# Retention and a bilinear FFN on one core: slots 6 to 23 transposed by DMA pair by pair, and two blocks of the first tile in 256-column halves

## The chip, the cores and the metric

The kernel runs on one core of a Trainium2 chip. The metric is the device time of one execution in microseconds; lower is better. Times of several runs are given by their median. A profile of one execution shows what each engine did: TensorE (PE, with its weight loads as PEld), VectorE (DVE), ScalarE (ACT), GpSimd (POOL), and SyncE (SP), which here issues nearly all DMAs.

## The reference

Two steps. A retention recurrence over 4 batches, 8 heads, 768 positions and head size 64, then a bilinear FFN over its 3072 rows of 512 columns.

```
state = gamma[h] * state + k_t (outer) v_t          # per batch and head, 64 x 64
y_t   = scale * q_t @ state
...
x   = y as [3072, 512]
out = ((x @ w_a) * (x @ w_b)) @ w_out               # w_a, w_b: 512 x 1536, w_out: 1536 x 512
```

Inputs and the output are float32.

## The kernel before, in words

**Slots and tiles.** The 3072 rows are 24 slots of 128 positions, 6 to a batch. The FFN works on tiles of slots, `TILES = [4, 2, 2, 2, 2, 4, 4, 4]`: the first tile is 512 columns wide (slots 0 to 3), the next four 256 (4 to 11), the last three 512. For a tile `J`, `ffn_a(J, ft)` and `ffn_g(J, ft)` compute one of 12 blocks of 128 rows of x @ w_a and x @ w_b, each with four matmuls (`KT`), into one PSUM bank; ACT copies the first into `asb` (L507), DVE multiplies the second by it into `ht` (L516). `ffn_out(J, i)` then makes the 128 output rows of slot `i` of the tile with 12 matmuls of 512 columns (L541), ACT copies them to `osb`, and a store is kept in `held`; `store()` issues it on SP at the start of the next FFN step.

**Retention.** It is computed in chunks of 64 positions. For each slot q and k are loaded (`load_slot`, L83; three DMAs of 256 KB on SP, for k, q and v), scaled with decay tables and cast to bf16 into `kqb` (`scaled`, L207, on POOL for slots from 6 on), and v is cast into `vb` (L224). q and k are then needed transposed, as `kqT`. Slots 0 to 5 take a path of their own (`casts2`, `flip2`, `scores2` and so on), which the change does not touch. For the slots from 6 on, `turn(new, old)` runs the retention of a pair of slots: the chunk states of the new pair (`chunk_states`, L264, which reads `kb` and `vb`), its scores (`scores`, L287, which reads `kqT`), and, for the pair before it, the part across chunks (`inter`, L328, which reads `kqT`) and within them (`intra`, L340, which reads `vb`), which make x for the FFN.

**Who transposes.** `ON_PE = 8`. Slots from 8 on are transposed by DMA: `casts(t)` issues the transpose on SP (L227) behind the scaling, and behind it on SP the three loads of slot t + 3 (L231). Slots 6 and 7 are transposed by TensorE: `flip(t)` runs eight transposes of 128x128, four for k and four for q (L236, L238), into a PSUM bank, and DVE copies the result into `kqT` (L240).

**Order.** Each engine's instructions run in the order in which they are written (`seq`), so each queue is one line of waiting. SP's first loads are the list `LOADS`: ten of its entries at the start, the rest (`issue_loads(100)`, L595) during the first tile, ending with slots 6, 7, 8, 9 and 10. The dictionary `ahead` (L636) says which of `casts`, `flip` and `turn` is written ahead of which FFN step: (1, 6) is block 6 of tile 1, (0, "o", 1) the second output block of tile 0. All 12 blocks of tile 1 come before the output blocks of tile 0, then those of tile 1, and from tile 2 on each tile's blocks are followed by its outputs.

**Buffers.** The raw loads of k, q and v lie in 3 buffers each, one to a pair of slots; `kqb`, `vb` and `kqT` have 6 each, so slot t takes over what slot t - 6 leaves; PSUM gives 3 banks to the tag `ff`, which the FFN blocks, the output blocks and `flip` share.

Of the kernel before, what the change touches and what calls it, by code (L numbers as in the profile page):

```python
# [10 lines left out]
BF16 = mybir.dt.bfloat16  # L11
# [3 lines left out]

TILES = [4, 2, 2, 2, 2, 4, 4, 4]
PAIRS = 3
ON_PE = 8


LOADS = "k0 q0 k1 q1 v0 v1 w0 w1 w2 w3 w4 k2 q2 v2 w5 o0 o1 o2 o3 o4 o5 s6 s7 s8 s9 s10".split()


@with_exitstack
def kernel(
# [10 lines left out]
    nc = tc.nc  # L36
    P = 128
    B, H, S, D = q.shape
    NCH = S // P
    HP = H // 2  # L40
    DM = H * D
    DFF = moe_w_a.shape[1]
    KT = DM // P
    NFT = DFF // P
    NSLOT = B * NCH
# [14 lines left out]
    tra = ctx.enter_context(tc.tile_pool(name="tra", bufs=4))  # L60
# [3 lines left out]
    psff = ctx.enter_context(tc.tile_pool(name="psff", bufs=3, space=bass.MemoryType.PSUM))  # L64
# [7 lines left out]
    def seq(bi):  # L72
        ins = bi.ins
        prev = last.get(ins.engine)
        if prev is not None:
            tc.add_manual_dep(ins, prev.name, nosync, reason="program order")
        last[ins.engine] = ins
        return bi


    raws, wst, whole = {}, {}, {}

    def load_slot(t):  # L83
        b, ci = divmod(t, NCH)
        for nm, src in (("k", k), ("q", q), ("v", v)):
            if t % 2 == 0:
                whole[nm] = raw.tile([P, 2, H, D], F32, tag=nm + "f", name=nm + "f")
            raws[nm, t] = whole[nm][:, t % 2]
            s = src[b, :, ci * P : (ci + 1) * P, :].rearrange("h p d -> p h d")
            seq(nc.sync.dma_start(out=raws[nm, t], in_=s))  # L90

    def load_pair(nm, u):
        src = {"k": k, "q": q, "v": v}[nm]
# [18 lines left out]

    pending = list(LOADS)

    def issue_loads(n):
        for _ in range(min(n, len(pending))):
            what = pending.pop(0)
            if what[0] in "kqv":
                load_pair(what[0], int(what[1:]))
            else:  # L120
                {"s": load_slot, "w": load_w, "o": load_o}[what[0]](int(what[1:]))
# [11 lines left out]
    ident = const.tile([P, P], BF16, name="ident")  # L133
# [43 lines left out]
    wa_bf = wpool.tile([P, KT, DFF], BF16, name="wa_bf")  # L177
    wb_bf = wpool.tile([P, KT, DFF], BF16, name="wb_bf")
    wo_bf = wpool.tile([P, NFT, DM], BF16, name="wo_bf")

    def cast(engine, dst, src):
        if engine is nc.scalar:
            seq(nc.scalar.copy(dst, src))  # L183
        else:
            seq(engine.tensor_copy(dst, src))  # L185
# [11 lines left out]
    kb, qb, vb, kqT, aT = {}, {}, {}, {}, {}  # L197
# [9 lines left out]
    def scaled(eng, t, i):  # L207
        ktab, qtab = tabs[0] if t < 2 * PAIRS else tabs[1]
        dst, src, tab = kqb[t][:, i], raws["kq"[i], t], (ktab, qtab)[i][:, t % NCH]
        dst = dst.rearrange("p hp r d -> p r hp d")  # L210
        src = src.rearrange("p (r hp) d -> p r hp d", r=2)
        tab = tab.rearrange("p (r hp) o -> p r hp o", r=2).to_broadcast([P, 2, HP, D])
        seq(eng.tensor_tensor(dst, src, tab, op=ALU.mult))  # L213

    def new_nat(t):
        kqb[t] = nat.tile([P, 2, HP, 2, D], BF16, tag="kqb", name="kqb")
        kb[t], qb[t] = kqb[t][:, 0], kqb[t][:, 1]
        vb[t] = nat.tile([P, H, D], BF16, tag="vb", name="vb")

    def casts(t):  # L220
        new_nat(t)
        scaled(nc.gpsimd, t, 0)
        scaled(nc.gpsimd, t, 1)
        cast(nc.gpsimd, vb[t], raws["v", t])  # L224
        if t >= ON_PE:
            kqT[t] = tra.tile([P, 2, HP, P], BF16, tag="kqT", name="kqT", bufs=6)
            seq(nc.sync.dma_start_transpose(  # L227
                out=kqT[t].rearrange("p a b c -> p (a b) c"),
                in_=kqb[t].rearrange("p a hp r d -> p (a hp r d)")))
            if t + 3 < NSLOT:  # L230
                load_slot(t + 3)  # L231

    def flip(t):
        tp = psff.tile([P, 2, HP, P], BF16, tag="ff", name="tp")
        for hp in range(HP):
            seq(nc.tensor.transpose(tp[:, 0, hp, :], kb[t][:, hp, :, :], ident))  # L236
        for hp in range(HP):
            seq(nc.tensor.transpose(tp[:, 1, hp, :], qb[t][:, hp, :, :], ident))  # L238
        kqT[t] = tra.tile([P, 2, HP, P], BF16, tag="kqT", name="kqT", bufs=6)
        seq(nc.vector.tensor_copy(kqT[t], tp))  # L240

    def half(i):
        return slice(64 * i, 64 * i + 64)
# [238 lines left out]
    def xcols(J, kt, c0, c1):  # L482
        if J < 2:
            return xt[J][:, c0 // P : c1 // P, kt, :]
        return xt[J][:, kt, c0:c1]
# [8 lines left out]

    asbs = {}

    def ffn_a(J, ft, c0=0, c1=None):
        c1 = TILES[J] * P if c1 is None else c1
        if J not in ht:
            ht[J] = htp.tile([P, NFT, 4 * P], BF16, tag="ht", name="ht")  # L500
        fs = slice(ft * P, (ft + 1) * P)
        a = psff.tile([P, 4 * P], F32, tag="ff", name="a")[:, : c1 - c0]
        for kt in range(KT):
            seq(nc.tensor.matmul(a, wa_bf[:, kt, fs], xcols(J, kt, c0, c1),  # L504
                                 start=(kt == 0), stop=(kt == KT - 1)))
        asb = asbs[J, ft, c0] = asbp.tile([P, 4 * P], BF16, tag="asb", name="asb")[:, : c1 - c0]
        seq(nc.scalar.copy(asb, a))  # L507

    def ffn_g(J, ft, c0=0, c1=None):
        c1 = TILES[J] * P if c1 is None else c1  # L510
        fs = slice(ft * P, (ft + 1) * P)
        g = psff.tile([P, 4 * P], F32, tag="ff", name="g")[:, : c1 - c0]
        for kt in range(KT):
            seq(nc.tensor.matmul(g, wb_bf[:, kt, fs], xcols(J, kt, c0, c1),  # L514
                                 start=(kt == 0), stop=(kt == KT - 1)))
        seq(nc.vector.tensor_tensor(ht[J][:, ft, c0:c1], g, asbs.pop((J, ft, c0)), op=ALU.mult))  # L516

    def ffn_ab(J, ft):
        store()
        ffn_a(J, ft)  # L520
        ffn_g(J, ft)
        catch_up(2)
# [67 lines left out]
    leave2(1, (A_, D_))  # L590
    W2 = 2 * P
    ffn_a(0, 0, 0, W2)
    update2(1, 1, False)
    ffn_a(0, 1, 0, W2)
    issue_loads(100)  # L595
    cast_w(1)
    ffn_g(0, 0, 0, W2)
    ffn_a(0, 0, W2, 2 * W2)
    ffn_a(0, 1, W2, 2 * W2)
    ffn_g(0, 1, 0, W2)  # L600
    ffn_g(0, 0, W2, 2 * W2)
    ffn_g(0, 1, W2, 2 * W2)
# [31 lines left out]
    for j in range(NO):  # L634
        cast_o(j)
    ahead = {  # L636
        (1, 6): [(casts, 6)], (1, 9): [(flip, 6), (casts, 7)], (0, "o", 0): [(flip, 7)],
        (0, "o", 1): [(turn, 6, None)], (0, "o", 2): [(casts, 8)], (0, "o", 3): [(casts, 9)],
        (1, "o", 1): [(turn, 8, 6, D_), (casts, 10)],
        (2, 2): [(casts, 11)], (2, 7): [(casts, 12)], (2, "o", 1): [(turn, 10, 8, D_), (casts, 13)],  # L640
        (3, 0): [(casts, 14)], (3, 6): [(casts, 15)], (3, "o", 0): [(turn, 12, 10), (casts, 16)],
# [58 lines left out]
```

## Time and profile before

| | |
|---|---|
| runs | 227.81 us median of 3 (227.33 to 228.07) |
| the profiled execution | 226.77 us, of it 225.1 us span from the first to the last instruction |
| granted TensorE clock | 1.000 |
| DMA | 39.20 MB, mean 174 GB/s over the span |

Engines overlap, so busy times don't add up to the span. The profile counts a matmul as busy until its modelled end, and matmuls are pipelined, so a group's own length is read from the starts of it and of what follows it. Weight loads (PEld) overlap matmuls. A row of the timeline gives the start and the length in us, the engine, the line of the kernel, the operation, what it writes and reads, the shape and a count; in square brackets stands how long the engine was idle ahead of it and what ended that.

### The profile page before, as it was taken

To read this page: it belongs to the slowest core of one execution; us is meant where nothing else is said; L and a number is where in the kernel's file an instruction comes from. 1 tells how busy PE (TensorE), PEld (TensorE's weight loads), DVE (VectorE), ACT (ScalarE), POOL (GpSimd) and SP (SyncE) were. 2 spreads that over 40 slices of the span, in tenths; PEclk is the share of its full clock that TensorE was granted. 3 is DMA by queue.
4 is the path that set the end of the run, shared out by engine and by line. 5 is a ranking of instruction groups with operands and counts; after the bars stand their busy time and mean duration, and the time that the engine had idled before them with its cause. 6 is when DMAs were issued, how large, how long until landed. Compare 5 with 4: busy or idle time off the path is not lost.

```text
span 225.1 us, 6289 instructions
## 1 busy us (share of the span) xinstructions
PE 218.3 (97%) x2632; PEld 131.5 (58%) x2632; DVE 97.4 (43%) x197; ACT 96.1 (43%) x206; POOL 80.0 (36%) x104
## 2 busy tenths in 40 slices
PE   7789999999999999999999999999999999999994
PEld 7567445796546867875885444545444544444444
DVE  3784347554506535462467243544243422333300
ACT  3465335332427326455447433355433354333222
POOL 5677799687544435417019510050000000000000
PEclk9999999999999999999999999999999999999999
DMA  6999999999999999999949893044100012100022
GB/s 186 347 380 382 364 309 406 303 241 219 208 288 231 298 152 207 265 237 167 287 113 206 184 248 67 3 96 143 47 0 0 3 50 93 47 3 1 1 93 93
DMA packets 94012, 39.20 MB, mean 174 GB/s; under 512 B 73888, under 2 KB 89504, under 8 KB 93984
## 3 DMA queue, kind: packets, MB, share of 16 engines
q1 hardware_dynamic: 93840, 38.68, 68.9%
q8 instruction: 20, 0.33, 0.6%
q10 hardware_dynamic: 144, 0.13, 0.2%
q14 instruction: 8, 0.07, 0.1%
HBM read 28.31 MB, written 6.29 MB: 154 GB/s over the span
## 4 chain that ended last, share of the span: by engine, by line
PE 92%; DMA 3%; ACT 1%; POOL 1%; issue 1%; SPq 0%; POOLq 0%
PE o L541 28%; PE g L514 28%; PE a L504 28%; DMA kf<-in_k_dram 3%; PE y L328 1%; POOL kqb L213 1%; PE at L287 1%; PE y L340 1%; PE st L264 1%; PE y L467 1%; PE y L455 1%; PE tp L402 0%; PE st L438 0%; SPq L96 0%; ACT qT L183 0%
## 5 line engine op out<-in xcount | busy, mean ns | idle before, releaser
L516 DVE TENSOR_TENSOR ht<-g,asb 128x256 bf16<-128x256 f32 (+1 forms) x98 | 53.9, 550 | 84.3 <-PE g L514 74.4
L514 PE MATMUL g<-xt,wb_bf 128*128 128x256 bf16 (+1 forms) x392 | 77.6, 323 | 0.1
L504 PE MATMUL a<-xt,wa_bf 128*128 128x256 bf16 (+1 forms) x392 | 77.6, 323 | 0.0
L507 ACT CAST asb<-a 128x256 bf16<-128x256 f32 (+1 forms) x98 | 46.4, 473 | 71.6 <-PE a L504 70.9
L541 PE MATMUL o<-wo_bf,ht 128*128 128x512 bf16 (+2 forms) x312 | 64.4, 363 | 0.0
L504 PEld LDWEIGHTS <-wa_bf 128*128 128x128 bf16 x392 | 38.0, 98 | 24.8 <-DVE xt L185 0.4
L514 PEld LDWEIGHTS <-wb_bf 128*128 128x128 bf16 x392 | 38.3, 98 | 23.9 <-issue 0.2
L541 PEld LDWEIGHTS <-ht 128*128 128x128 bf16 x312 | 28.8, 98 | 30.5
L213 POOL TENSOR_TENSOR kqb<-kf,ktab 128x512 bf16<-128x512 f32 x22 | 22.9, 1045 | 22.3 <-DMA kf<-in_k_dram 19.7
L183 ACT COPY osb<-o 128x512 f32<-128x512 f32 (+2 forms) x25 | 14.1, 565 | 33.4 <-PE o L541 28.1
L185 POOL CAST vb<-vf 128x512 bf16<-128x512 f32 x24 | 14.5, 613 | 38.0 <-PE y L340 24.8
L213 POOL TENSOR_TENSOR kqb<-qf,qtab 128x512 bf16<-128x512 f32 x21 | 22.4, 1067 | 1.8 <-DMA qf<-in_q_dram 1.7
L183 ACT CAST gst<-sums 128x256 bf16<-128x256 f32 x33 | 13.4, 405 | 6.1 <-DVE sums L278 2.8
L278 DVE TENSOR_TENSOR sums<-st,sums 128x256 f32<-128x256 f32 x30 | 12.7, 424 | 1.6
L293 DVE TENSOR_TENSOR aT<-at,mask 128x512 bf16<-128x512 f32 x18 | 11.5, 679 | 0.0
L351 ACT CAST xt<-y 128x512 bf16<-128x512 f32 x16 | 8.5, 584 | 0.0
L490 PE MATMUL idle<-zero 128*128 128x170 bf16 (+1 forms) x56 | 7.2, 295 | 1.1 <-DVE zero L127 1.1
L425 DVE TENSOR_TENSOR aT<-at,mask 128x512 bf16<-128x512 f32 x12 | 7.4, 678 | 0.7 <-PE at L415 0.7
L185 POOL CAST wa_bf<-wsta 128x1024 bf16<-128x1024 f32 (+1 forms) x7 | 6.4, 922 | 2.7 <-DMA wsta<-in_moe_w_a_dram 2.6
L185 POOL CAST wb_bf<-wstb 128x1024 bf16<-128x1024 f32 (+1 forms) x7 | 6.4, 922 | 1.4 <-DMA wstb<-in_moe_w_b_dram 1.4
L185 POOL CAST wo_bf<-wsto 128x1024 bf16<-128x1024 f32 x6 | 6.3, 1044 | 1.7 <-DMA wsto<-in_moe_w_out_dram 0.9
L305 DVE COPY lgr<-bq 128x1 f32<-128x1 f32 x4 | 0.6, 154 | 14.2 <-PE y L328 14.2
(58 smaller groups left out, 95.1 us busy)
## 6 DMA issues: line engine op xcount, KB each, us to landing
out_dram<-osb SPq DMA_DIRECT2D x23, 256.0 KB, 3.4
kf<-in_k_dram SPq DMA_DIRECT2D x18, 256.0 KB, 4.1
qf<-in_q_dram SPq DMA_DIRECT2D x18, 256.0 KB, 4.1
vf<-in_v_dram SPq DMA_DIRECT2D x18, 256.0 KB, 4.5
wsta<-in_moe_w_a_dram SPq DMA_DIRECT2D x6, 512.0 KB, 7.7
wstb<-in_moe_w_b_dram SPq DMA_DIRECT2D x6, 512.0 KB, 7.8
wsto<-in_moe_w_out_dram SPq DMA_DIRECT2D x6, 512.0 KB, 7.8
kf<-in_k_dram SPq DMA_DIRECT2D x3, 512.0 KB, 5.8
```

The source lines that it names most:

```text
L183: seq(nc.scalar.copy(dst, src))
L185: seq(engine.tensor_copy(dst, src))
L213: seq(eng.tensor_tensor(dst, src, tab, op=ALU.mult))
L278: seq(nc.vector.tensor_tensor(new, u[c][:, s], old, op=ALU.add))
L293: seq(nc.vector.tensor_tensor(aT[n][:, r].rearrange("p s h d -> p (s h) d"), at[:, r].rearrange("p s h d -> p (s h) d"), mask.to_broadcast ...
L351: seq(nc.scalar.copy(dst, ys[o][c]))
L425: seq(nc.vector.tensor_tensor(aT[t][:, r], ats[t][r], masks[par].to_broadcast([P, HP, P]), op=ALU.mult))
L504: seq(nc.tensor.matmul(a, wa_bf[:, kt, fs], xcols(J, kt, c0, c1), start=(kt == 0), stop=(kt == KT - 1)))
L507: seq(nc.scalar.copy(asb, a))
L514: seq(nc.tensor.matmul(g, wb_bf[:, kt, fs], xcols(J, kt, c0, c1), start=(kt == 0), stop=(kt == KT - 1)))
L516: seq(nc.vector.tensor_tensor(ht[J][:, ft, c0:c1], g, asbs.pop((J, ft, c0)), op=ALU.mult))
L541: seq(nc.tensor.matmul(o, ht[J][:, ft, i * P : (i + 1) * P], wo_bf[:, ft, c0:c1], start=(ft == 0), stop=(ft == NFT - 1)))
```

## The change

`ON_PE` and `flip` go; `casts` issues a DMA transpose for slots 6 and 7 too. The first list of loads ends with slot 7. From then on the loads go by pairs: behind the transpose of an odd slot t, SP gets the loads of k and q of slots t + 1 and t + 2, then those of v. `load_slot` and `casts` take the names of what they are to handle, and slots 8 and 9 have k and q of both scaled ahead of v. In `casts` the loop over `("kq", "v")` uses the variable `names` again. In `ahead`, slot 7 moves from (1, 9) to (1, 8). For blocks 2 and 3 of the first tile each matmul of 512 columns becomes two of 256, into the two halves of the same bank.

```
-LOADS = "k0 q0 k1 q1 v0 v1 w0 w1 w2 w3 w4 k2 q2 v2 w5 o0 o1 o2 o3 o4 o5 s6 s7 s8 s9 s10".split()
+LOADS = "k0 q0 k1 q1 v0 v1 w0 w1 w2 w3 w4 k2 q2 v2 w5 o0 o1 o2 o3 o4 o5 s6 s7".split()
...
-    def load_slot(t):
+    def load_slot(t, names="kqv"):
         b, ci = divmod(t, NCH)
-        for nm, src in (("k", k), ("q", q), ("v", v)):
+        for nm in names:
...
+    def casts(t, names="kqv"):
+        if "k" in names:
+            new_nat(t)
+            scaled(nc.gpsimd, t, 0)
+            scaled(nc.gpsimd, t, 1)
             kqT[t] = tra.tile([P, 2, HP, P], BF16, tag="kqT", name="kqT", bufs=6)
             seq(nc.sync.dma_start_transpose(
                 out=kqT[t].rearrange("p a b c -> p (a b) c"),
                 in_=kqb[t].rearrange("p a hp r d -> p (a hp r d)")))
-            if t + 3 < NSLOT:
-                load_slot(t + 3)
+            if t % 2 and t + 1 < NSLOT:
+                for names in ("kq", "v"):
+                    load_slot(t + 1, names)
+                    load_slot(t + 2, names)
+        if "v" in names:
+            cast(nc.gpsimd, vb[t], raws["v", t])
...
+    def parts(J, ft, c0, c1):
+        if J == 0 and ft in (2, 3):
+            return [(c0, (c0 + c1) // 2), ((c0 + c1) // 2, c1)]
+        return [(c0, c1)]
...
         for kt in range(KT):
-            seq(nc.tensor.matmul(a, wa_bf[:, kt, fs], xcols(J, kt, c0, c1),
-                                 start=(kt == 0), stop=(kt == KT - 1)))
+            for b0, b1 in parts(J, ft, c0, c1):
+                seq(nc.tensor.matmul(a[:, b0 - c0 : b1 - c0], wa_bf[:, kt, fs], xcols(J, kt, b0, b1),
+                                     start=(kt == 0 and b0 == c0), stop=(kt == KT - 1 and b1 == c1),
+                                     skip_group_check=True))
...
-        (1, 6): [(casts, 6)], (1, 9): [(flip, 6), (casts, 7)], (0, "o", 0): [(flip, 7)],
-        (0, "o", 1): [(turn, 6, None)], (0, "o", 2): [(casts, 8)], (0, "o", 3): [(casts, 9)],
+        (1, 6): [(casts, 6)], (1, 8): [(casts, 7)], (0, "o", 1): [(turn, 6, None)],
+        (0, "o", 2): [(casts, 8, "kq")],
+        (0, "o", 3): [(casts, 9, "kq"), (casts, 8, "v"), (casts, 9, "v")],
```

`ffn_g` is changed as `ffn_a` is.

More of the change, by code (lines that the diff above doesn't have):

```diff
@@ L17 @@
 PAIRS = 3
-ON_PE = 8
-LOADS = "k0 q0 k1 q1 v0 v1 w0 w1 w2 w3 w4 k2 q2 v2 w5 o0 o1 o2 o3 o4 o5 s6 s7 s8 s9 s10".split()
+LOADS = "k0 q0 k1 q1 v0 v1 w0 w1 w2 w3 w4 k2 q2 v2 w5 o0 o1 o2 o3 o4 o5 s6 s7".split()
 @with_exitstack
@@ L88, in load_slot @@
             raws[nm, t] = whole[nm][:, t % 2]
-            s = src[b, :, ci * P : (ci + 1) * P, :].rearrange("h p d -> p h d")
-            seq(nc.sync.dma_start(out=raws[nm, t], in_=s))
+            s = {"k": k, "q": q, "v": v}[nm][b, :, ci * P : (ci + 1) * P, :]
+            seq(nc.sync.dma_start(out=raws[nm, t], in_=s.rearrange("h p d -> p h d")))
     def load_pair(nm, u):
@@ L218, in new_nat @@
         vb[t] = nat.tile([P, H, D], BF16, tag="vb", name="vb")
[L220 to L225, printed above, removed]
+    def casts(t, names="kqv"):
[3 more added lines that the diff above has]
+            scaled(nc.gpsimd, t, 1)
             kqT[t] = tra.tile([P, 2, HP, P], BF16, tag="kqT", name="kqT", bufs=6)
@@ L229, in casts @@
                 in_=kqb[t].rearrange("p a hp r d -> p (a hp r d)")))
-            if t + 3 < NSLOT:
-                load_slot(t + 3)
[L233 to L240, printed above, removed]
+            if t % 2 and t + 1 < NSLOT:
[4 more added lines that the diff above has]
+            cast(nc.gpsimd, vb[t], raws["v", t])
     def half(i):
@@ L513, in ffn_g @@
         for kt in range(KT):
-            seq(nc.tensor.matmul(g, wb_bf[:, kt, fs], xcols(J, kt, c0, c1),
-                                 start=(kt == 0), stop=(kt == KT - 1)))
+            for b0, b1 in parts(J, ft, c0, c1):
+                seq(nc.tensor.matmul(g[:, b0 - c0 : b1 - c0], wb_bf[:, kt, fs], xcols(J, kt, b0, b1),
+                                     start=(kt == 0 and b0 == c0), stop=(kt == KT - 1 and b1 == c1),
+                                     skip_group_check=True))
         seq(nc.vector.tensor_tensor(ht[J][:, ft, c0:c1], g, asbs.pop((J, ft, c0)), op=ALU.mult))
```

## The prediction

> **What bounds the kernel now.** I read the page first: span, busy shares, the slices and the chain of work that ended last.
>
> ```profile
> span 225.1 us, 6289 instructions
> PE 218.3 (97%) x2632; PEld 131.5 (58%) x2632; DVE 97.4 (43%) x197; ACT 96.1 (43%) x206; POOL 80.0 (36%) x104
> ...
> PE   7789999999999999999999999999999999999994
> ...
> PEclk9999999999999999999999999999999999999999
> DMA  6999999999999999999949893044100012100022
> ...
> PE 92%; DMA 3%; ACT 1%; POOL 1%; issue 1%; SPq 0%; POOLq 0%
> ```
>
> TensorE sets the end: it is busy in every slice from the fourth on, its granted clock is full throughout, and the chain is 92% PE. The transfers are busy too, up to about 112 us (the first 20 slices of 5.63 us), but the chain has only 3% of them, all at the start. The view of busy time by windows says the same for the stretch that the change touches:
>
> ```profile
> 42.00:50.00 8.00, 8.00 (x76) 7.10 (x75) 4.09 (x9) 3.36 (x9) 6.24 (x7) 1.00 1.05 239
> 50.00:57.00 7.00, 7.00 (x118) 4.89 (x116) 3.39 (x7) 1.70 (x4) 5.20 (x6) 1.00 1.02 229
> ...
> 85.00:121.00 36.00, 36.00 (x679) 27.46 (x667) 19.03 (x44) 18.98 (x49) 14.21 (x17) 1.00 1.01 209
> ```
>
> The columns are length, busy time of PE, PEld, DVE, ACT and POOL, clock, DMA share, GB/s. PE is busy for all of each window; no other engine reaches 80% on the same terms, save the weight loads, which overlap. So what leaves PE's stream leaves the end, unless a new wait takes its place.
>
> **The change, part by part.** *The 16 transposes of slots 6 and 7 leave PE* (L236, L238). The timeline of PE shows what they take:
>
> ```profile
> 49.81 0.39 PE L236 MATMUL tp<-ident,kqb 128*128 128x128 bf16 x4
> 50.04 0.39 PE L238 MATMUL tp<-ident,kqb 128*128 128x128 bf16 x4
> 50.26 0.60 PE L504 MATMUL a<-xt,wa_bf 128*128 128x256 bf16 x4
> ...
> 52.95 0.39 PE L236 MATMUL tp<-ident,kqb 128*128 128x128 bf16 x4
> 53.17 0.39 PE L238 MATMUL tp<-ident,kqb 128*128 128x128 bf16 x4
> 53.39 2.75 PE L541 MATMUL o<-wo_bf,ht 128*128 128x512 bf16 x12
> 56.08 0.45 PE L264 MATMUL st<-vb,kqb 64*64 64x64 bf16 x32
> 56.35 0.49 PE L287 MATMUL at<-kqT 64*64 64x64 bf16 x32
> ```
>
> Matmuls are pipelined, so starts count, not durations: 50.26 - 49.81 = 0.45 and 53.39 - 52.95 = 0.44, together 0.89 us off PE. The Trainium skill, "TensorE: Matmul & The Clock Gate", section on the PE-mode transpose, puts a 128x128 transpose at about 275 ns in one kernel's context; by that the 16 would be worth an estimated 4.4 us. The starts above stand 56 ns apart, so the trace disagrees and I go by it.
>
> Their two copies on DVE (0.69 us each) leave too. That is worth nothing on the path: DVE is busy 3.39 of 7.00 us there.
>
> ```profile
> L240 DVE COPY kqT<-tp 128x1024 bf16<-128x1024 bf16 x2 | 1.4, 690 | 0.0
> ```
>
> *Halves.* The blocks ft = 2 and 3 of the first tile run 16 matmuls of 512 columns (a and g, 4 each); they become 32 of 256. Both widths stand side by side:
>
> ```profile
> 18.78 1.04 PE L504 MATMUL a<-xt,wa_bf 128*128 128x256 bf16 x8
> 19.65 1.47 PE L514 MATMUL g<-xt,wb_bf 128*128 128x256 bf16 x12
> 20.96 1.89 PE L504 MATMUL a<-xt,wa_bf 128*128 128x512 bf16 x8
> 22.69 1.89 PE L514 MATMUL g<-xt,wb_bf 128*128 128x512 bf16 x8
> ```
>
> 256 columns: (20.96 - 19.65) / 12 = 109 ns. 512 columns: (22.69 - 20.96) / 8 = 216 ns. Two halves cost 218 ns against 216: 16 x 2.6 ns = 0.04 us more. Each half has a weight load of its own (98 ns), which 109 ns still covers. If none of the 16 added loads were covered, they would cost 1.57 us; that is the upper bound, 0 the lower; I take 0.04, since the same form runs at that pace just before.
>
> ```profile
> L504 PEld LDWEIGHTS <-wa_bf 128*128 128x128 bf16 x392 | 38.0, 98 | 24.8 <-DVE xt L185 0.4 <-issue 0.2
> ```
>
> Sum on PE: -0.89 + 0.04 = -0.85 us. Everything else has to stay hidden, and that is the question.
>
> *Slots 6 and 7 by DMA.* The queue SP now issues the transpose of slot 6 (T6) right behind the loads of slot 7, T7 next, and only then the loads of 8 and 9 (k8 q8 k9 q9 v8 v9). T6 and T7 wait for POOL's scaling, and k8 to v9 are queued behind them. The rows of POOL, of SP, and of the transposes before:
>
> ```profile
> 45.40 1.04 POOL L213 TENSOR_TENSOR kqb<-qf,qtab 128x512 bf16<-128x512 f32 x1
> ...
> 48.19 1.04 POOL L213 TENSOR_TENSOR kqb<-qf,qtab 128x512 bf16<-128x512 f32 x1
> 49.18 0.61 POOL L185 CAST vb<-vf 128x512 bf16<-128x512 f32 x1
> ```
> ```profile
> 44.72 0.93 SPq L90 DMA_DIRECT2D vf<-in_v_dram  x1
> ```
> ```profile
> L227 SPq DMA_TRANSPOSE kqT<-kqb x10: 1288/1378/1862, 57.3 to 107.7; - x10
> ...
> DMA to landing us min/median/max: 3.7/4.4/5.5
> ```
>
> SP is free of slot 7's loads at 45.7. q6 is scaled at 46.4, q7 at 49.2; a transpose takes SP 1.4 us and lands 4.4 us (5.5 at most) after its issue starts, in the crowded stretch from 57 to 112 us. So T7 lands at 49.3 + 4.4 = 53.7 (54.8 at most). Its first reader is the score group L287 at 56.35, 0.85 earlier after the change: 55.5. Slack 1.8 us, 0.7 at the worst. Cost 0; without that cover, each us of lateness is a us of PE.
>
> *Slots 8 and 9.* Before, T9 was issued at 62.91. Its new predecessors: loads from 50.7 on. A load lands 4.1 us after issue, and the next ones follow at 0.262 MB / 233 GB/s = 1.13 us each (both from the stretch 57 to 112 us, the loads of k and the summary of the DMA queues):
>
> ```profile
> 62.91 1.33 SPq L227 DMA_TRANSPOSE kqT<-kqb  x1
> ```
> ```profile
> DMA to landing us min/median/max: 3.3/4.1/5.1
> ```
> ```profile
> DMA packets 42462, 12.80 MB, mean 233 GB/s; under 512 B 41303, under 2 KB 41303, under 8 KB 42455
> ```
> ```profile
> 59.62 0.59 ACT L183 COPY osb<-o 128x512 f32<-128x512 f32 x1 [0.71 <-PE o L541]
> 67.68 0.45 PE L287 MATMUL at<-kqT 64*64 64x64 bf16 x32
> ```
>
> k8 lands at 54.8, q9 at 54.8 + 3.4 = 58.2, scaled at 59.2 (1.04 us, the rows of POOL above). T9 also stands behind the store of the second output block, which waits for ACT's copy: 59.62 + 0.59 - 0.85 = 59.4. So T9 is issued at 59.4 and lands at 63.8 (64.9), 3 us before its reader (67.68 - 0.85 = 66.8). In `casts` the loop variable overwrites `names`, so slot 9's v is cast a second time: one more 0.61 us on POOL, where POOL stands idle for 3.00 us:
>
> ```profile
> 63.06 1.04 POOL L213 TENSOR_TENSOR kqb<-kf,ktab 128x512 bf16<-128x512 f32 x1 [3.00 <-DMA kf<-in_k_dram]
> ```
>
> *The later pairs.* Loads ran three slots ahead; now a pair's six are issued behind the last transpose of the pair before, so one link hangs on the next: transpose issue 1.4, first load 4.1, four more (q, k, q, v) 4 x 1.13 = 4.5, then POOL's v, k and q 0.61 + 1.04 + 1.04 = 2.7: 12.7 us a pair. From T9 at 59.4, T17 is issued four links on at 110.2 and lands at 114.6. The readers of slots 10, 12, 14 and 16 are
>
> ```profile
> 84.77 0.44 PE L287 MATMUL at<-kqT 64*64 64x64 bf16 x29
> ...
> 99.19 0.49 PE L287 MATMUL at<-kqT 64*64 64x64 bf16 x32
> ...
> 116.29 0.49 PE L287 MATMUL at<-kqT 64*64 64x64 bf16 x32
> ...
> 120.22 0.21 PE L287 MATMUL at<-kqT 64*64 64x64 bf16 x1
> ```
>
> For slots 16 and 17 that is 120.22 - 0.85 = 119.4, slack 4.8 us over four links, the least of all per link (slots 10 to 15: 83.9 - 76.5 = 7.4 over one, 98.3 - 89.2 = 9.1 over two, 115.4 - 101.9 = 13.5 over three). Cost 0. Its bound the other way: 1.86 for the issue, 5.1 to land, 4 x 0.262 MB / 209 GB/s = 5.0 at the pace of the window 85 to 121, and 2.7 make 14.7 a link; T17 then lands at 59.4 + 58.8 + 5.5 = 123.7, and PE stands for 4.3 us.
>
> The sum: the span becomes 225.1 - 0.85 = 224.25, the profiled execution 226.77 - 0.85 = 225.9. The runs shown have their median 1.04 us above that execution, so 227.81 - 0.85 = 226.96, said as 226.95.
>
> **The rivals.** *The chain of pairs is too long (slower).* The place is the turn of slots 16 and 17 at 119.4. It decides from (119.4 - 59.4 - 4.4) / 4 = 13.9 us a link; each us above costs PE four, and above 14.1 the whole is slower. At the bound of 14.7, 4.3 us: 231.3. For it: the transfers stand at 9 in every slice up to 112 us, so a link may meet stores and transposes in the queue. Against: that load was made by running ahead, and 12.7 leaves 1.2 us a link. Chance 0.08.
>
> *The halves expose their weight loads.* 1.57 instead of 0.04: 227.81 - 0.89 + 1.57 = 228.5. Against: 12 matmuls of that form at 109 ns. Chance 0.08.
>
> *The gain is swallowed by a wait at the next hand-over.* T7, T9 or a cast comes 0.85 us later than PE can use it, past the worst case above, by a delay that the rows don't show: 227.8. For it: T7's slack at the worst is only 0.7. Against: the DMA queue is emptier than before once three slots' loads are gone from it. Chance 0.13.
>
> *The transposes cost more than their starts say.* One by itself takes 0.39 - 3 x 0.056 = 0.22 us (four take 0.39, started 56 ns apart); if what follows had to wait for each to drain, the 16 would be worth 3.5 us: 227.81 - 3.5 + 0.04 = 224.35. Against: the next block's first matmul starts 0.22 us after the second four, as if they flowed on. Chance 0.03. By the page's 275 ns it would be 227.81 - 4.4 + 0.04 = 223.45, which the same row speaks against.
>
> **How the numbers follow.** The forecast has 0.68, and its own range is 226.5 to 227.4: 0.85 with some 0.4 either way for the spread of the runs before (227.33 to 228.07). A measurement here tells about 0.3%, 0.68 us, from no change, and 0.85 is just beyond it. So of the 0.68 I count 0.56 as faster by more than that, 0.11 as within, 0.01 as slower; of the swallowed gain 0.06 within and 0.07 slower; the first two rivals are slower, 0.16, the last faster, 0.03. Faster 0.59, same 0.17, slower 0.24. The range, 226.3 to 228.4, holds nearly all of the forecast and of the swallowed gain and reaches to the exposed halves at 228.5 without all of it; the long chain lies outside.
>
> **What would show it.** Right: no L236 and L238, 18 transposes on SP, the score group of slots 6 and 7 starting 0.8 to 0.9 us earlier with no PE idle before it, and the same lead at 66.8, 84, 98, 115 and 119 us. The halves are right if the 16 blocks of 256 columns start 109 ns apart. The chain is right if T17 lands before 119 us. Wrong: idle time of PE ahead of an L287 or an L264, put down to a transpose's landing or to a cast of vb, or a lead that shrinks from one turn to the next.

## The result and the profile after

The changed kernel takes 226.56 us, median of 10 runs (226.02 to 227.02); the kernel before, run beside it, 227.38 (226.92 to 228.07, 10 runs). The ratio is 0.9964 [0.9949, 0.9978], so the change gains 0.82 us. Ratios leave out runs more than 1.5% above the fastest of their kernel; one run further down, of 233.13 us, is such. The profiled execution of the changed kernel took 226.44 us. Its page:

```profile
span 224.7 us, 6284 instructions
PE 217.7 (97%) x2632; PEld 132.3 (59%) x2632; DVE 96.2 (43%) x195; ACT 96.0 (43%) x206; POOL 80.3 (36%) x105
...
PEclk9999999999999999999999999999999999999999
DMA  6999999998899996999979996974100012100022
...
q8 instruction: 20, 0.33, 0.6%
...
PE 92%; DMA 3%; ACT 1%; POOL 1%; issue 1%; SPq 0%; POOLq 0%
```

The picture is that of before: PE fills the span at full clock, and the chain is 92% PE. PE has the same 2632 matmuls, since 16 transposes went and 16 matmuls came. DVE has two instructions less (the copies of the transposes), POOL one more (the second cast of slot 9's v). The line of q8, a queue that carries instructions, matters further down: 20 packets with 0.33 MB, 16 KB each.

The timeline of PE around the place where the transposes were (columns: start, length, engine, line, operation, tiles, shape, count):

```profile
49.46 0.60 PE L516 MATMUL g<-xt,wb_bf 128*128 128x256 bf16 x4
49.90 0.60 PE L504 MATMUL a<-xt,wa_bf 128*128 128x256 bf16 x4
...
52.08 0.60 PE L516 MATMUL g<-xt,wb_bf 128*128 128x256 bf16 x4
52.52 2.75 PE L544 MATMUL o<-wo_bf,ht 128*128 128x512 bf16 x12
55.20 0.45 PE L257 MATMUL st<-vb,kqb 64*64 64x64 bf16 x32
55.47 0.49 PE L280 MATMUL at<-kqT 64*64 64x64 bf16 x32
```

The FFN blocks follow each other 0.44 us apart without a gap, and the scores of slots 6 and 7 start at 55.47 instead of 56.35: a lead of 0.88 us. The same timeline further on, at the scores (L280) of the later pairs and at the chunk states (L257) of the last:

```profile
66.81 0.45 PE L280 MATMUL at<-kqT 64*64 64x64 bf16 x32
...
98.43 0.49 PE L280 MATMUL at<-kqT 64*64 64x64 bf16 x32
...
115.52 0.49 PE L280 MATMUL at<-kqT 64*64 64x64 bf16 x32
...
119.10 0.32 PE L321 MATMUL y<-kqT,gst 64*64 64x64 bf16 x16
119.30 0.67 PE L257 MATMUL st<-vb,kqb 64*64 64x64 bf16 x20
...
119.86 0.42 PE L280 MATMUL at<-kqT 64*64 64x64 bf16 x28
```

The rows of the kernel before at the last of these turns:

```profile
119.87 0.32 PE L328 MATMUL y<-kqT,gst 64*64 64x64 bf16 x16
120.05 0.35 PE L264 MATMUL st<-vb,kqb 64*64 64x64 bf16 x19
...
120.30 0.44 PE L287 MATMUL at<-kqT 64*64 64x64 bf16 x28
```

Against the rows of before the lead is 0.87 at 66.81, 0.76 at 98.43, 0.77 at 115.52, and 120.30 - 119.86 = 0.44 at the last one. So 0.1 us was lost at the turn of slots 10 and 11 and 0.3 at the turn of 16 and 17. There the chunk states take 0.67 us for 20 matmuls, where the kernel before took 0.35 for 19, and no wait is recorded with them. These leads are counted from the start of the span; the first FFN matmul starts at 17.02 here and at 16.98 before. Counted from that matmul on, the lead is 0.92 at the scores of slots 6 and 7, and PE's last matmul starts 0.49 us earlier than before; a second execution of the changed kernel has 0.55.

The halves, in the same timeline:

```profile
21.00 1.91 PE L504 MATMUL a<-xt,wa_bf 128*128 128x256 bf16 x16
22.75 1.91 PE L516 MATMUL g<-xt,wb_bf 128*128 128x256 bf16 x16
24.49 1.67 PE L504 MATMUL a<-xt,wa_bf 128*128 128x512 bf16 x7
```

(22.75 - 21.00) / 16 = 109 ns each, as in the rows of before.

The timeline of SP, from slot 7's transpose to slot 17's:

```profile
50.34 1.23 SPq L225 DMA_TRANSPOSE kqT<-kqb  x1
...
57.22 3.04 SPq L531 DMA_DIRECT2D out_dram<-osb  x1
60.35 1.31 SPq L225 DMA_TRANSPOSE kqT<-kqb  x1
61.76 0.53 SPq L531 DMA_DIRECT2D out_dram<-osb  x1
62.38 1.31 SPq L225 DMA_TRANSPOSE kqT<-kqb  x1
...
75.27 1.26 SPq L225 DMA_TRANSPOSE kqT<-kqb  x1
...
99.51 1.26 SPq L225 DMA_TRANSPOSE kqT<-kqb  x1
...
112.36 1.24 SPq L225 DMA_TRANSPOSE kqT<-kqb  x1
```

T7 goes out at 50.34 and lands 3.2 us later (the view of that line gives the landing) at 53.5, 2.0 us ahead of its reader. T9 goes out at 62.38, lands at 65.4, 1.4 us ahead. T17 goes out at 112.36, lands at 115.8, 4.1 us ahead. No score group waits for a transpose.

So the open questions were: is it the transposes that bring the gain, and the order of the loads that covers them; what do the halves do; how much room has the chain of pairs; and what is the stop at the turn of 16 and 17?

### The profile page after: what moved, and what is told of

Read it like the earlier page. It is cut to its first block, busy times and chain, and to the rows that moved or that the text cites. A ratio compares the mean times of both kernels' runs of the same rounds, so it can differ in the third digit from the quotient of the medians.

```text
span 224.7 us, 6284 instructions
## 1 busy us (share of the span) xinstructions
PE 217.7 (97%) x2632; PEld 132.3 (59%) x2632; DVE 96.2 (43%) x195; ACT 96.0 (43%) x206; POOL 80.3 (36%) x105
## 4 chain that ended last, share of the span: by engine, by line
PE 92%; DMA 3%; ACT 1%; POOL 1%; issue 1%; SPq 0%; POOLq 0%
PE o L544 28%; PE g L516 28%; PE a L504 28%; DMA kf<-in_k_dram 3%; PE y L321 1%; POOL kqb L212 1%; PE at L280 1%; PE y L333 1%; PE st L257 1%; PE y L460 1%; PE y L448 1%; PE tp L395 0%; PE st L431 0%; SPq L95 0%; ACT qT L182 0%
## 5 line engine op out<-in xcount | busy, mean ns | idle before, releaser
L504 PEld LDWEIGHTS <-wa_bf 128*128 128x128 bf16 x400 | 38.8, 98 | 24.0 <-DVE xt L184 0.4
L516 PEld LDWEIGHTS <-wb_bf 128*128 128x128 bf16 x400 | 39.1, 98 | 23.1 <-issue 0.2
L271 DVE TENSOR_TENSOR sums<-st,sums 128x256 f32<-128x256 f32 x30 | 12.7, 424 | 1.9 <-PE st L257 0.4
```

Source lines behind the costliest of these rows:

```text
L271: seq(nc.vector.tensor_tensor(new, u[c][:, s], old, op=ALU.add))
L504: seq(nc.tensor.matmul(a[:, b0 - c0 : b1 - c0], wa_bf[:, kt, fs], xcols(J, kt, b0, b1), start=(kt == 0 and b0 == c0), stop=(kt == KT - 1 a ...
L516: seq(nc.tensor.matmul(g[:, b0 - c0 : b1 - c0], wb_bf[:, kt, fs], xcols(J, kt, b0, b1), start=(kt == 0 and b0 == c0), stop=(kt == KT - 1 a ...
```

## The experiments: what the gain is made of

Theory: TensorE loses 16 transposes, worth 0.88 us, and the new order of loads is only cover for the two DMA transposes. Rivals: the new order of loads or the halves bring the gain.

**The DMA transposes without the new order.** The kernel before, with slots 6 and 7 transposed by DMA, the loads as they were.

```
-        if t >= ON_PE:
+        if True:
...
-            if t + 3 < NSLOT:
+            if t >= ON_PE and t + 3 < NSLOT:
...
-        (1, 6): [(casts, 6)], (1, 9): [(flip, 6), (casts, 7)], (0, "o", 0): [(flip, 7)],
+        (1, 6): [(casts, 6)], (1, 8): [(casts, 7)],
```

> The kernel before, with slots 6 and 7 transposed by DMA and nothing else moved: the loads of slots 8, 9 and 10 stay ahead of the two transposes in SP's queue, the blocks stay whole. Theory (the transposes are the gain, the order of the loads is their cover): SP is through with those loads at 55.9 us, so T6 is issued there and T7 some 1.5 us later, T7 lands at about 61.5 to 62; the scores of slots 6 and 7 want it at 55.5, so PE stands for some 6 us and the kernel is about 5 us slower than before (+4 to +6.5). Rival (the transposes are worth 0.85 us wherever they stand in the queue): 0.85 us faster than before. Rival (the order of the loads makes the gain, not the transposes): within 0.3 us of before.

Measured: 233.94 us (233.25 to 234.97), ratio 1.0309 [1.0282, 1.0335], 7.0 us slower, more than the 4 to 6.5 expected. Its SP and PE timelines:

```profile
54.50 1.60 SPq L90 DMA_DIRECT2D vf<-in_v_dram  x1
56.20 3.06 SPq L227 DMA_TRANSPOSE kqT<-kqb  x2
```
```profile
55.69 0.45 PE L264 MATMUL st<-vb,kqb 64*64 64x64 bf16 x32
60.23 0.43 PE L287 MATMUL at<-kqT 64*64 64x64 bf16 x16 [4.10 <-DMA kqT<-kqb]
61.07 0.43 PE L287 MATMUL at<-kqT 64*64 64x64 bf16 x16 [0.41 <-DMA kqT<-kqb]
```

Both transposes stand on SP behind the nine loads of slots 8 to 10, go out at 56.2, and PE stands for 4.10 + 0.41 us. The cover is thus the place in the queue. But 4.5 us of standing cost 7.0, in a kernel that also lost the 16 transposes. The windows of this run show one part of the rest (length, busy time of PE, PEld, DVE, ACT, POOL, then the granted clock):

```profile
58.00:60.30 2.30, 0.07 (x4) 0.07 (x8) 0.07 (x1) 0.46 (x2) 1.80 (x3) 0.52 1.28 224
60.30:62.00 1.70, 1.29 (x33) 0.80 (x35) 0.45 (x1) 0.00 (x0) 0.00 (x0) 0.50 1.10 288
62.00:64.00 2.00, 1.78 (x6) 0.64 (x5) 0.84 (x2) 0.00 (x0) 0.00 (x0) 0.50 0.73 164
64.00:66.00 2.00, 2.00 (x9) 0.86 (x8) 0.00 (x0) 0.02 (x1) 1.44 (x2) 0.77 1.13 255
```

The clock is at half some 2 us after PE stopped (56.1), and stays there to about 65, well into the work: (1.7 + 2.0) x 0.50 + 2.0 x 0.23 = 2.3 us more. 4.5 + 2.3 - 0.9 = 5.9 us. That is all that this trace has: counted from the first FFN matmul on, PE's last matmul starts 5.79 us later than before. The rest of the 7.0 lies outside this stretch: the profiled execution took 233.25, the shortest of the four, and its first FFN matmul started at 17.55, 0.57 us later than before.

**The new order without the DMA transposes.** The kernel before with the loads by pairs, slots 6 and 7 still transposed by TensorE (the `flip` entries stay in `ahead`), whole blocks. The order of scalings of slots 8 and 9 is that of the changed kernel.

```
-LOADS = "k0 q0 k1 q1 v0 v1 w0 w1 w2 w3 w4 k2 q2 v2 w5 o0 o1 o2 o3 o4 o5 s6 s7 s8 s9 s10".split()
+LOADS = "k0 q0 k1 q1 v0 v1 w0 w1 w2 w3 w4 k2 q2 v2 w5 o0 o1 o2 o3 o4 o5 s6 s7".split()
...
+            if t >= 8:
...
+            if t % 2 and t + 1 < NSLOT:
+                for names in ("kq", "v"):
+                    load_slot(t + 1, names)
+                    load_slot(t + 2, names)
```

> The kernel before with the loads pair by pair as in the changed kernel, but slots 6 and 7 transposed on PE and the blocks whole. Theory (the loads' order is only cover): within 0.1 us of before, or up to 0.4 us slower if the losses of the changed kernel's profile at the turns at 84 and 119 us belong to the chain of pairs. Rival (the order of the loads is the gain): 0.5 to 0.9 us faster than before.

Measured: 227.31 us (226.9 to 227.92, 12 runs), before 226.96, ratio 1.0011 [1.0001, 1.0022]. In its profile PE's last matmul starts 0.34 us later than before, and a stop of 0.27 us lies at the turn of slots 16 and 17, in the same place as in the changed kernel. So the order by pairs brings nothing by itself. By the ratio it costs some 0.25 us (0.02 to 0.5), which the prediction had at 0. From this kernel to the changed one with whole blocks (226.45 us, run beside it, next section) little else moves than the 16 transposes, from TensorE to DMA, with their copies on DVE gone and slot 7's casts one step earlier. The medians differ by 0.86 us. That is the most direct measurement of what the transposes are worth.

**The two kernels again.** The changed kernel and the kernel before, each once more without an edit.

> The changed kernel itself, beside the others. Theory: 0.85 us off PE less what the order by pairs gives back (the kernel before with the loads by pairs alone was 0.35 us slower by its medians): 0.4 to 0.9 us faster than before. If PE stands about 0.3 us at the second matmul of the chunk states of slots 16 and 17 again, as in the first profile and in that of the loads by pairs alone, that loss belongs to the order by pairs and not to one execution.

> The kernel before once more, for a second trace of it. Theory: within 0.2 us of before; T9 lands 0.5 to 1.5 us ahead of the scores of slots 8 and 9, no stop of PE at the turn of slots 16 and 17, and the first block of the FFN starts between 16.9 and 18 us, by as much as it did in the other traces, so that about 0.3 us and more of a single run's time is the start and not the kernel.

Measured: changed 226.67 us (226.42 to 228.37), ratio 0.9979 [0.9952, 1.0006]; before 227.29 (226.85 to 227.54), ratio 1.0009 [0.9998, 1.0019]. The stop at the turn of 16 and 17 is back in the changed kernel (0.29 us, at the same matmul) and absent in the one before. In two executions of each it goes with the kernel.

The other loss does not. At the turn of slots 10 and 11 the second profile of the kernel before loses 0.15 us too, as its rows show beside those of the first:

```profile
85.18 0.51 PE L340 MATMUL y<-aT,vb 64*64 64x64 bf16 x32
```
```profile
85.39 0.66 PE L340 MATMUL y<-aT,vb 64*64 64x64 bf16 x32
```

So the 0.1 us there can't be put down to the order by pairs. Against this second profile, counted from the first FFN matmul on, the two profiles of the changed kernel are 0.64 and 0.70 us ahead at the end.

## The experiments: the halves

**The changed kernel with whole blocks**, twice:

```
-        if J == 0 and ft in (2, 3):
+        if False:
```

> The changed kernel with blocks 2 and 3 of the first tile whole again. Theory (the halves cost 16 x 2.6 ns): 0.04 us faster than the changed kernel, not to be told from it: 0.8 to 0.9 us faster than before. Rival (the halves carry a part of the gain): less than 0.5 us faster than before. Rival (the halves expose weight loads): 1.2 us or more faster than before. In its profile the lead over the trace of before is 0.89 to 0.95 us at the first output block; whether the two losses of the changed kernel's profile (0.1 us at 84 us, 0.3 us at 119 us) come again tells if they belong to the kernel or to that execution.

> The changed kernel with whole blocks once more, beside the same kernel with 16 idle matmuls more. Theory: 0.6 to 0.9 us faster than before, and 0.2 to 0.4 us faster than that one. Rival: the two are alike.

Measured: 226.45 us (226.11 to 226.72), ratio 0.9974 [0.9962, 0.9985], and 226.45 (226.23 to 227.16), ratio 0.9979 [0.997, 0.9988]. PE's last matmul starts 0.91 us earlier than before in the first. In the second it starts only 0.10 us earlier: a stop of 0.46 us lies at the turn of 16 and 17, and 0.4 us more is lost at other turns. That execution took 227.16, the longest of its eleven. The two medians lie 0.51 and 0.56 us below the kernel before, a little less than the 0.8 and 0.6 us expected at the least. By their times neither can be told from the changed kernel: the halves bring nothing that can be measured, and cost nothing.

**The halves alone**, in the kernel before (`parts` and the two loops over it, as in the diff of the change).

```
+    def parts(J, ft, c0, c1):
+        if J == 0 and ft in (2, 3):
+            return [(c0, (c0 + c1) // 2), ((c0 + c1) // 2, c1)]
+        return [(c0, c1)]
...
+            for b0, b1 in parts(J, ft, c0, c1):
```

> The kernel before with blocks 2 and 3 of the first tile in halves and nothing else. Theory: 0.04 us slower than before, not to be told from no change (ratio 0.999 to 1.001). Rival (the halves are a part of the gain): 0.3 us or more faster. Rival (exposed weight loads): up to 1.57 us slower.

Measured: 228.48 us (228.22 to 228.77), ratio 1.0066 [1.0054, 1.0079]: 1.5 us slower, where 0.04 was expected. That is the price of the rival in which all weight loads of the halves are exposed (1.57), but not its place. In the profile 0.04 us is lost up to the scores of slots 6 and 7, as foretold for the halves; the rest is lost from slot 8 on, 0.78 us first at the scores of slots 8 and 9:

```profile
67.74 0.32 PE L287 MATMUL at<-kqT 64*64 64x64 bf16 x16
68.68 0.32 PE L287 MATMUL at<-kqT 64*64 64x64 bf16 x16 [0.62 <-DMA kqT<-kqb]
...
100.39 0.98 PE L340 MATMUL y<-aT,vb 64*64 64x64 bf16 x32
```

T9 landed late, and the last row, 32 small matmuls in 0.98 us instead of 0.53, has a stop of 0.34 us with no wait recorded. Another of 0.35 us lies in the second output block behind the turn of slots 16 and 17, at 124.87. What the halves change at all after 25 us is one thing: every later instruction of PE stands 32 places further on in its stream (16 matmuls, 16 weight loads). The next kernel moves the stream by as much without halves.

**The kernel before with 16 more idle matmuls at the start**, narrower ones, so that together they take as long:

```
-    warm(36, psat, "y1", 170)
+    warm(52, psat, "y1", 118)
```

> The kernel before, whole blocks, with 16 more matmuls on PE, but not as halves: the 36 idle matmuls of 170 columns at the start become 52 of 118, the same columns and about the same time, ahead of the first data. Every later PE instruction moves 32 places back in PE's stream, as in the kernel before with halves alone (1.5 us slower). Theory (halves cost next to nothing; what that kernel lost came of moving the stream, so that refills of PE's instructions over the DMA queue fall elsewhere, delay the transpose of slot 9 and stop PE in the turns): 0.8 to 1.8 us slower than before, with the losses at the turns at 68, 82 and 121 us as in that kernel. Rival (the halves themselves cost 1.5 us there, by their weight loads or otherwise): within 0.3 us of before.

Measured: 229.06 us (four runs from 228.57 to 229.44, and one of 233.13), ratio 1.0088 [1.0075, 1.0102], 2.0 us slower, with no change to any block. That is a little more than the 0.8 to 1.8 expected, and it is lost at 102 and 125.6 us, not at the turns at 68, 82 and 121 us that were expected. Its PE timeline at the turn of slots 14 and 15:

```profile
99.64 0.51 PE L340 MATMUL y<-aT,vb 64*64 64x64 bf16 x30
102.06 0.22 PE L340 MATMUL y<-aT,vb 64*64 64x64 bf16 x2 [1.92 <-issue]
```

One stop of 1.92 us in the middle of a group whose inputs were there, put down to "issue". It is the place of the 0.34 us in the kernel with the halves alone: row 2750 of PE's stream in both, counted in the order of the program. The second stop, of 0.20 us at 125.59, lies in the same output block as with the halves. T9 came in time here, so its lateness in the profile with the halves, a little under half of that kernel's loss, is another matter, left open. But that moving the stream by 32 places costs this kernel 2.0 us, without halves, is shown.

**The changed kernel with whole blocks and the 16 idle matmuls**, so that the stream stands where it stands with the halves:

> The changed kernel with whole blocks and the same 16 idle matmuls more at the start, so that PE's stream stands from the first turn on where it stands in the changed kernel. Theory (the 0.3 us at the second matmul of the turn of slots 16 and 17 is a refill of PE's instructions that comes late): that loss is back at the same matmul, and the lead of PE's stream over the trace of before is 0.5 to 0.6 us at the end of that turn, where the whole blocks alone had 0.9. Rival (the loss hangs on the halves): it stays away.

Measured: 226.47 us (226.1 to 228.42), before 227.01, but the ratio is 0.9995 [0.9975, 1.0015]; median and ratio don't agree, and the time decides nothing. In the profile a stop of 0.20 us is back at the matmul where the changed kernel has it. But the lead at the end is 0.78 us, not the 0.5 to 0.6 expected, and the whole blocks without idle matmuls, run beside it, have the same time (226.45) and a stop as well. There the stop lies at the same row of the stream, at another matmul. So the comparison of these two settles nothing; what speaks is the row.

## What the stop is

PE runs 5264 instructions, 2632 matmuls and as many weight loads, and q8 brings 20 packets of 16 KB: one for each 256 or so. The stops without a recorded wait of 0.2 us and more, from slot 8 on, lie at rows 3260 (changed kernel, twice; whole blocks, second time; whole blocks with idle matmuls), 3262 (pairs alone), 2750 and 3516 (both in the kernel with the halves alone and in that with idle matmuls). Divided by 256 all leave 188 to 190, whichever matmul stands there: a fixed place of a page of the stream, a page being 256 rows.

All fourteen profiles bear this out. There are 19 such places, from row 444 to row 5052, and the packet that belongs to one is the packet of the same number. In no profile does PE get past such a place less than 1.33 us after the end of its packet; at the nine stops it does so 1.35 to 1.64 us after it.

The Trainium skill, "Runtime: NRT & Kernel Launch", section "Instruction fetch mechanics", says that an engine's instructions are refilled in blocks of 16 KiB, 256 instructions, and that crossing a block costs little that is not hidden. The 16 KB and the 256 agree with the rows here; "mostly hidden" does not hold for the 1.92 us above.

Eight profiles have row 3260 at the same matmul, a chunk state of the turn of 16 and 17. The table gives, from each trace, when the q8 packet before it starts and ends, counted from the first `inter` matmul (L328 before, L321 changed) of the turn before (115.89 in the kernel before, 115.12 in the changed one), the DMA rate in the stretch from 0.9 to 3.9 us on the same count, and the stop.

| kernel | packet starts, us | ends, us | GB/s | stop, us |
|---|---|---|---|---|
| before | 1.04 | 2.29 | 93 | none |
| before again | 0.98 | 2.11 | 93 | none |
| changed, links longer by one cast (next section) | 1.04 | 2.29 | 117 | none |
| changed, links longer by two scalings (next section) | 1.34 | 2.45 | 62 | none |
| changed | 1.97 | 2.85 | 261 | 0.3 |
| pairs alone | 2.11 | 2.99 | 262 | 0.27 |
| changed, whole blocks and 16 idle matmuls | 2.08 | 3.01 | 249 | 0.20 |
| changed again | 2.14 | 3.09 | 239 | 0.29 |

Where the transfers are quiet, the packet goes out 1.0 us into the count and PE doesn't stop (in the fourth row they run only in the first third of the stretch, and the packet goes out 1.3 us into the count); where the loads of slots 18 and 19 fill the queue, it goes out 1 us later and PE stops. The summaries of DMA in that stretch, of the kernel before and of the changed one, carry the difference in one line each:

```profile
DMA packets 1057, 0.28 MB, mean 93 GB/s; under 512 B 1056, under 2 KB 1056, under 8 KB 1056
```
```profile
DMA packets 3036, 0.78 MB, mean 261 GB/s; under 512 B 3035, under 2 KB 3035, under 8 KB 3035
```

In the cases with a stop, PE goes on 1.35 to 1.64 us after the packet ends (119.61 after 117.97 in the changed kernel). The third and fourth rows are the telling ones: their PE instructions are those of the changed kernel, only their loads come later. So the order by pairs puts its loads where the order before left the queue empty, and PE's next page is late by what it then takes. This is one execution of each kernel; that the loads delay the packet is read from eight of them, not tried by itself.

The stop at row 2750 follows its packet in the same way: in the kernel with the idle matmuls the packet ends at 100.64, and PE goes on 1.4 us later. It took 1.72 us, and around it the transfers of data come nearly to a standstill, shown here for 98.9 to 100.7 us in 40 slices:

```profile
GB/s 541 154 131 114 199 199 256 262 273 216 91 74 17 17 11 0 0 0 0 0 0 0 0 0 0 0 0 0 0 0 0 0 0 0 0 0 0 0 6 11
DMA packets 390, 0.12 MB, mean 64 GB/s; under 512 B 389, under 2 KB 389, under 8 KB 389
```

Here PE's part of the delay is plain and its cause is not. Such pauses stand beside refills elsewhere too: one in the changed kernel, from 59.6 to 60.7 us, begins at the end of a refill (57.74 to 59.65) and covers the last part of the store that kept SP for 3.04 us, above. Whether the refill makes the pause or both hang on a third thing was not found out.

## The experiments: the room of the chain

**The loads one slot ahead of the transposes.** The changed kernel, whole blocks, from slot 10 on each transpose followed by the loads of slot t + 2; slot 9's v is cast once.

```
-            if t % 2 and t + 1 < NSLOT:
-                for names in ("kq", "v"):
-                    load_slot(t + 1, names)
-                    load_slot(t + 2, names)
+            if t in (7, 9):
+                for part in ("kq", "v"):
+                    load_slot(t + 1, part)
+                    load_slot(t + 2, part)
+            elif 10 <= t < NSLOT - 2:
+                load_slot(t + 2)
```

> The changed kernel with whole blocks, without the second cast of slot 9's v, and from slot 10 on with the loads of slot t + 2 behind each transpose of slot t, where the changed kernel waits for a pair. Theory (the order by pairs has room enough and nothing waits for it but the 0.3 us at the turn of slots 16 and 17): T17 lands at 111 us or earlier instead of 115.8, and the time is 0.85 to 0.95 us faster than before. Rival (the chain is not what that 0.3 us hangs on): the loss at that turn stays and the time equals that of the changed kernel.

Measured: 226.74 us (226.07 to 227.56, 12 runs), ratio 0.9981 [0.9967, 0.9995]. T17 goes out at 110.20, 2.2 us earlier, and lands at 114.3 (111 was expected), and its PE stream keeps a lead of 0.87 us to the end without a stop. The time is no better, 0.4 us below the kernel before by the ratio where 0.85 was expected. The profiled execution was the longest of the twelve, 227.56; its first FFN matmul started 1.3 us late (18.30, where the other profiles have 16.96 to 17.55), and its granted clock was lower ahead of it, in the third slice of its page:

```profile
PEclk9969999999999999999999999999999999999999
```

That fits the late start of this execution; why the median is no better stays open.

**One more cast of v in each of four links** (0.61 us on POOL at slots 10, 12, 14 and 16), and **two more scalings in each** (2.08 us at slots 11, 13, 15 and 17):

```
+            if t in (10, 12, 14, 16):
+                cast(nc.gpsimd, vb[t], raws["v", t])
```
```
+            if t in (11, 13, 15, 17):
+                scaled(nc.gpsimd, t, 0)
+                scaled(nc.gpsimd, t, 1)
```

> The changed kernel with one more cast of v (0.61 us on POOL, the same data again) in each of the four links of the chain between the transposes of slots 9 and 17. Theory (a link has about 1 us of room: T17 landed at 115.8 and is wanted at 119.4 to 119.8): T17 lands at some 118.2, still in time, and the time is that of the changed kernel within 0.3 us. Rival (the chain is already on the edge): 2 us or more slower than the changed kernel.

> The changed kernel with two more scalings (2.08 us on POOL, the same data again) in each of the four links between the transposes of slots 9 and 17. Theory (T17 has 3.6 to 4.0 us of room, and what is over it is PE's loss one for one): T17 lands 8.3 us later, at 124, and PE stands 4.3 to 4.7 us ahead of the scores of slots 16 and 17; 3.4 to 4.0 us slower than before. Rival (something else bounds the links, the DMA queue for one, and takes the added work up): less than 2 us slower than before.

Measured: 226.53 us (226.29 to 226.73), ratio 0.9964 [0.9945, 0.9984] for the cast; 230.95 (230.42 to 232.72), ratio 1.0181 [1.0149, 1.0213] for the scalings. T17 in the two, and what PE did in the second:

```profile
115.61 1.24 SPq L225 DMA_TRANSPOSE kqT<-kqb  x1
```
```profile
118.56 1.24 SPq L228 DMA_TRANSPOSE kqT<-kqb  x1
```
```profile
122.93 0.43 PE L283 MATMUL at<-kqT 64*64 64x64 bf16 x16 [2.92 <-DMA kqT<-kqb]
```

With the cast T17 goes out 3.2 us later (2.4 was put in) and lands at 119.7, 0.2 us ahead of its reader, and nobody waits. With the scalings it goes out 6.2 us later (8.3 was put in; where the rest went was not followed) and PE stands 2.92 us, where 4.3 to 4.7 was expected. So the room is between 3.2 and 6.2 us, as the 4.1 us from landing to reader say. The time rose by 4.3 us over the changed kernel run beside it (226.67), not by 2.9. Again the clock is the rest:

```profile
120.00:123.00 3.00, 0.08 (x5) 0.07 (x8) 1.20 (x3) 1.22 (x3) 0.00 (x0) 0.90 0.89 199
123.00:125.00 2.00, 2.00 (x67) 1.31 (x68) 1.29 (x2) 0.96 (x2) 1.49 (x2) 0.50 0.95 215
125.00:127.00 2.00, 2.00 (x8) 0.79 (x7) 0.00 (x0) 0.11 (x1) 0.55 (x1) 0.79 1.16 263
```

2.0 x 0.50 + 2.0 x 0.21 = 1.4 us; 2.9 + 1.4 = 4.3.

None of the versions beats the changed kernel beyond doubt. Whole blocks (226.45, twice) and the longer links (226.53) stand within the runs of the changed one.

## Why the prediction was right, point by point

**The sum on PE was right to 0.1 us.** 0.89 us was worked out for the transposes and 0.04 for the halves, -0.85 together; counted from the first FFN matmul, the lead at the scores of slots 6 and 7 is 0.92, and 0.96 with whole blocks. The difference is a delay of 0.06 us that the prediction did not see: in the kernel before, behind the first eight transposes, two blocks start 0.50 us apart (50.70 and 51.20) where the others start 0.44 apart. It is gone with the transposes; its cause is open. The 16 cost the 56 ns that their starts showed, neither their drained time nor the 275 ns of the Trainium skill, "TensorE: Matmul & The Clock Gate", Part 4. The halves at 109 ns were right too.

**The cover of T7 was right**: issue 49.3 foretold and 50.34 seen, landing 53.7 and 53.5, reader 55.5 and 55.47. That the landing fits so well is luck: the issue came 1.0 us late, since POOL scaled q7 from 49.27 on and not from 48.19 on, and the way to the landing took 3.2 us and not 4.4. T6 was issued at 46.63 and took 6.1 us, more than the 5.5 given as the most, and still landed at 52.7. The first experiment shows that it is the order on SP that makes it.

**T9 came nearer to its reader than foretold.** The step "So T9 is issued at 59.4" took the time of the store and of T8 on SP for nothing. POOL was done with q9 at 59.5, 0.3 us after the time foretold, but the store kept SP from 57.22 for 3.04 us, and T8 (1.31) and the next store (0.53) went ahead of T9 too. Of the 3 us of slack 1.4 were left. It cost nothing.

**The link was right.** 12.7 us foretold; from the four transposes at 62.38, 75.27, 99.51 and 112.36 it is (112.36 - 62.38) / 4 = 12.5. T17 landed at 115.8, 114.6 was foretold. The rival of the long chain fell as worked out, and its threshold holds: 0.8 us more a link (3.2 / 4) cost nothing, 1.55 more (6.2 / 4) did. Its price was too low, as was "each us of lateness is a us of PE": the stops of 2.9 and 4.5 us each halved the clock for what followed.

**What the prediction missed** is the cost of the new order, put at 0: the 0.3 us of a late refill. One of its own signs of being wrong appeared, a lead that shrinks from one turn to the next (0.92, 0.80, 0.49, counted from the first FFN matmul). It looked for waits on data, and this stop has none. The 0.1 us at the turn of slots 10 and 11 is lost by the kernel before as well, in one of its two profiles. In the two profiles of the changed kernel PE's end is 0.49 and 0.55 us ahead of the first profile of before, and 0.64 and 0.70 ahead of the second, not 0.85. The runs can't tell these: the medians give 0.82 and 0.64, and the intervals hold 0.5 as well as 0.85. So the mechanism is shown, its size to some 0.3 us, and that the first median came within 0.03 us of the forecast gain is partly luck.

**The level.** 226.95 was said from a median of 227.81 over three runs; over ten runs the kernel before has 227.38, and of the 0.39 us between 226.95 and 226.56 the base is 0.43.

## What to carry to other kernels

When TensorE bounds a kernel, work that leaves its stream is worth about the distance between starts, and a DMA that takes its place needs a place in its queue ahead of the later loads: the same transposes behind nine loads cost 7 us. Before an added instruction is blamed for a loss, run a control that moves the engine's stream by as many places without it. And in looking for what an emptier or fuller DMA queue does, count the instruction packets among what it may hold up.

## What was not expected of the hardware

**Instruction refills can stop PE.** In a run of 64x64 matmuls PE uses its instructions fast (in the timeline of the kernel before, the turn of 16 and 17, 128 matmuls with their weight loads, takes from 119.87 to 121.14), and in and right behind such runs stops of 0.2 to 1.9 us lie at one place of the 256-row page. Adding 32 instructions at the start of the kernel, which themselves cost nothing (the first FFN matmul starts at 16.96 instead of 16.98), made it 2.0 us slower.

**Two long stops of PE cost more than themselves.** In windows of half a us the granted clock falls to 0.50 about 2.0 us into the stop of the first experiment and 2.4 us into that of the longer links, and comes back after some 4.5 and 3 us of work. The stop of 1.92 us left it at 1.00; where between these the change lies was not measured. The Trainium skill, "TensorE: Matmul & The Clock Gate", Part 1, has the clock go to half after an idle window of about 3.4 us that runs freely; half is what the rows show, though it came here after 2.0 and 2.4 us of standing.
